# Clustered attention and a mixture of experts on one core: nine small transfers by another queue, and four edits to the plan

## The chip, the cores and the metric

The kernel runs on one core of a Trainium2 chip. A core has five engines with a queue of instructions each: TensorE (PE, matmuls), VectorE (DVE), ScalarE (ACT), GpSimd (POOL) and SyncE (SP, which here only starts transfers). Each queue is worked in order; an instruction that waits holds up everything behind it on its engine. Sixteen DMA engines move the data of all transfers. The metric is the device time of one execution in microseconds (us), the median over several runs.

## The reference, cut to what matters

The first part is attention over 4 batches, 8 heads, 768 tokens and 64 features. Each query and each key is put into one of 16 clusters, and a query sees only the keys of its own cluster. The second part sends each of the 3072 tokens to 2 of 8 experts.

```python
q_assign = argmax(q_n . c_n);  k_assign = argmax(k_n . c_n)
mask = q_assign[:, :, :, None] == k_assign[:, :, None, :]
scores = where(mask, scale * q @ k.T, -1e9)
attn = softmax(scores, axis=-1)            # the row maximum is subtracted first
x = (attn @ v).transpose(0, 2, 1, 3).reshape(3072, 512)
logits = x @ w_gate + log1p(exp(x @ w_noise)) * noise
out[token] += w[token, e] * (relu(x[token] @ w1[e]) @ w2[e])   # for the 2 best e
```

## The kernel before, in words

**Pairs.** The 32 (batch, head) matrices are worked as 16 pairs of heads, called pair 0 to 15 by the code (the first pair is pair 0). For each pair one wide operand `A` and one `B` are put together in SBUF: 128 rows that hold the high and low halves of q and k, the one-hot cluster masks in rows 64 to 79 of `A`, and the row maxima in two rows of `B`. There are three buffers of each, used in turn (`A_152`, `A_153`, `A_154` and `B_155`, `B_156`, `B_157` in the order of the instructions).

**What makes a pair ready.** `a_split` (L414 to L424) turns q and k on PE, ACT writes the high half and DVE the low half, into a tile that is called `hl` (for pair 1 `xt`). `b_place` (L490) moves the halves into `A` and `B` with ten transfers. `a_sims` to `a_eq` (L435 to L471) find the clusters, `a_mask` (L480, L482) turns them on PE and lets ACT write the mask `mk`, and `b_mask` (L502) moves `mk` into `A` with four transfers. `b_max` (L516, L519) then makes the row maxima on PE and DVE, `b_neg` (L526 to L528) joins them in `nm`, and `b_negT` (L530) turns `nm` on PE, lets ACT copy the turned maxima to `nt` and moves `nt` into `B`. For pair 0 `b_neg` and `b_negT` run once for each head, for all other pairs once for both.

**What uses it.** `scores` (L547, L548) makes one step of 128 keys: two matmuls of `A` and two of `B`, and ACT's exponential `pe`. POOL makes the low half `pl` (L559), and `values` (L580 to L586) multiplies with v four steps later. DVE scales the pair's result into `xp` (L594); for the first pair `x_first` (L627), `x_hi` (L647, ACT) and `x_lo` (L651, POOL) halve it, `x_put` (L656) stores it in DRAM and `x_turn` (L663) turns it by a transposing transfer.

**The order.** All of this is recorded step by step. A table of numbers, `AT`, gives for each piece of work the step at which it is recorded; a step is one `scores` call, twelve to a pair, and negative steps lie ahead of the first scores. What is recorded first stands first on each queue. All transfers but the gathers are started by SP through one helper, `dma` (L487), or by `nc.sync` itself. Each transfer on these queues also waits for the transfer that was recorded eight before it, whichever queue starts it, because eight completion counters are used in turn.

**Experts.** Expert by expert, `layer1` (L1267) and `layer2` (L1305) follow. While expert 0 is at work, the weights of expert 1 are loaded, DVE takes their maxima (`max_w1`, L1185), and `w1_scale` (L1163 to L1174) makes a common scale from them, with one matmul of PE in each of its two parts.

Of the kernel before, what the change touches and what calls it, by code (L numbers as in the profile page):

```python
# [9 lines left out]
F32 = mybir.dt.float32  # L10
# [19 lines left out]
    vscale=-0.667, vsplit=10.667, vstep=1.0, split=[-4.667, -3.667, -4.0, -3.333], place=-0.667,  # L30
# [1 line left out]
    bmax=9.333, neg=20.333, negT=22.0, zero=31.0, zstep=12.0, zlist=15.667, store=2.667, log=1.667, log2=3.0,  # L32
    logstep=0.667, turn=7.667, list=23.0, lstep=[2.0, 2.0, 1.0], bstep=1.0,
    gate=7.667, gstep=0.333, am=5.333, amstep=0.333, ky=4.0, cut=[13, 20], gplace=17.333,
    vd=[1, 1, 2, 3, 4, 5], sec=-6.0, qf=-4.0, place1=4.333,
    fv=[{'v': -5.0, 'vscale': 13.0, 'am': 24.333, 'amstep': 0.333, 'vsplit': 25.333, 'vstep': 2.0},
        {'v': 9.0, 'vscale': 11.667, 'am': 13.333, 'amstep': 0.333, 'vsplit': 15.0, 'vstep': 1.667}],
    thr=0.333, bmax1=14.667, bstep1=0.5)
# [6 lines left out]
class Kernel:  # L45
# [154 lines left out]
    def attention(self, ctx):  # L200
        nc, tc = self.nc, self.tc
# [17 lines left out]
        def at(step, f, *a):  # L219
            sched.setdefault(divmod(round(3 * step), 3), []).append((f, a))  # L220

        def chain(step, by, fs):
            for i, f in enumerate(fs):
                at(step + by * i, f)
# [3 lines left out]
        for p in range(NP):  # L228
            b, hp = divmod(p, H // 2)
            w = 12 * (p - 2)  # L230
            if hp == 0:
                for g in range(2):
                    at(w + T["qk"] + 24 * g + (T["qf"] if (b, g) == (0, 1) else 0), self.load_qk, b, g)
                    v = w + 24 * g
                    V = T["fv"][g] if p == 0 else T
                    at(18.667 if (b, g) == (1, 0) else v + V["v"], self.load_v, b, g)
                    for h in range(0, 4, 2):
                        at(v + V["vscale"] + V["amstep"] * h, self.v_max, b, g, h)
                    chain(v + V["am"], V["amstep"], self.v_scale(b, g))
                    for h in range(4):  # L240
                        at(v + V["vsplit"] + V["vstep"] * h, self.v_split, b, g, h)
            if p == 0:
                at(17.333, self.x_first)
            for i in range(2 if p <= NP - 4 else 0):
                hi, lo = (18.667 + 1.333 * i, 20.0 + 1.333 * i) if p == 0 else (w + 38 + 3.667 * i, w + 39.333 + 3.667 * i)
                at(hi, self.x_hi, p, i)
                at(lo, self.x_lo, p, i)
                if i:
                    at(w + 45 if p else 21.667, self.x_put, p, i)
                    if p < NP - 4:  # L250
                        at(w + 46.667 if p else 21.667, self.x_turn, p)
            P = T["first"] if p == 0 else T
            w += (0, T["sec"], T["thr"])[p] if p < 3 else 0
            for i in range(4):
                at(w + P["split"][i], self.a_split, p, i // 2, i % 2)
            if p == 0:
                at(w + P["sims"][0], self.c_turn)
            at(w + P["place"] + (T["place1"] if p == 1 else 0), self.b_place, p)
            for s in range(2):
                at(w + P["sims"][s], self.a_sims, p, s)  # L260
            for s in range(2):
                at(w + P["sum"][s], self.a_sum, p, s)
            for k, f in (("max1", self.a_max1), ("ge", self.a_ge), ("ky", self.a_ky), ("max2", self.a_max2),
                         ("eq", self.a_eq), ("mask", self.a_mask), ("bmask", self.b_mask)):
                at(w + P[k], f, p)
            if p == 0:
                for s in range(2):
                    for j in range(NJ):
                        at(w + P["bmax"][s] + P["bstep"][s] * j, self.b_max, p, s, j)
                    at(w + P["neg"][s], self.b_neg, p, s, 1)  # L270
                    at(w + P["negT"][s], self.b_negT, p, s, 1)
            else:
                w = 12 * (p - 2)
                bm, bs = (T["bmax1"], T["bstep1"]) if p == 1 else (T["bmax"], T["bstep"])
                for s in range(2):
                    for j in range(NJ):
                        at(w + bm + bs * (6 * s + j), self.b_max, p, s, j)
                at(w + T["neg"], self.b_neg, p, 0, 2)
                at(w + T["negT"], self.b_negT, p, 0, 2)
            if hp == H // 2 - 1:  # L280
                z = w + 36 + L
                if b + 1 == B:
                    continue
                at(z + (10 if b == B - 2 else 14), self.g_halves, b)
                at(z + (11 if b == B - 2 else 14.667), self.g_turn, b)
                fs = self.g_gate(b)
                k = b == B - 2
                chain(z + (13 if k else 15.333), T["gstep"] / (1 + k), fs[:self.GP])
                chain(z + (19.333 if k else 26), T["gstep"] / (1 + k), fs[self.GP:])
                for j in range(2 * NJ):  # L290
                    at(z + ((22.333 if j < 1 else 24.667 + 0.333 * j) if k else T["list"] + 8.667 + T["lstep"][b] * j), self.g_list, b, j)
# [33 lines left out]
        for t in range(min(sched)[0], z + L + 2):  # L325
# [8 lines left out]
            if 0 <= u < z:  # L334
                p, s, kc = u // 12, (u % 12) // 6, u % 6
# [148 lines left out]
        st["mk"] = mk  # L484


    def dma(self, o, i):  # L487
        self.nc.sync.dma_start(o.bitcast(F32), i.bitcast(F32))

    def b_place(self, p):  # L490
        hl, A, Bt = self.st[p]["hl"], self.A[p % 3], self.Bt[p % 3]
# [10 lines left out]
    def b_mask(self, p):  # L502
        mk, A = self.st[p]["mk"], self.A[p % 3]
        for i in range(2):
            for a in range(2):
                self.dma(A[64:80, i, :, 384 * a:384 * a + 384], mk[64 * i + 32 * a:64 * i + 32 * a + 16])

    def b_max(self, p, s, j):

# [20 lines left out]
    def b_negT(self, p, s, n):  # L530
        nc, W = self.nc, 2 * n * self.NJ
        t = self.ps()
        nc.tensor.transpose(t[:, :128], self.nm.bitcast(F32), self.ident)
        nt = self.wk.tile([32, 128], F32R, name="nt")
        nc.scalar.activation(nt[:W], t[:W, :128], AF.Copy)
        self.dma(self.Bt[p % 3][96:98, 1, s:s + n], nt[:W])


    def scores(self, p, s, kc):
# [361 lines left out]
    def experts(self, ctx):  # L901
        nc, tc, E, DM, F, N, CAP, T, TA = self.nc, self.tc, self.E, self.DM, self.F, self.N, self.CAP, self.T, self.TA
        ND, NF, NJ, b = DM // 128, F // 128, self.NJ, self.B - 1
# [8 lines left out]
        A = (0, TA * 128)  # L912
# [68 lines left out]
                self.max_w1(1, t - 1)  # L981
        self.max_w1(1, 3)
        for f in range(NF):
            if 1 <= f < 3:
                self.w1_scale(1, f - 1)
            self.prep_w2(1, f - 5)
            self.prep_x(1, f - 3)
            self.layer1(0, f, [Bs])
# [5 lines left out]
        n = CAP // 2  # L994
        for e in range(1, E):
# [5 lines left out]
            for f in range(NF):  # L1001
# [7 lines left out]
                i = f - 1 if e > 1 else f - 3  # L1009
# [355 lines left out]
```

## Time and profile before

| | |
|---|---|
| median of 3 runs | 1060.86 us (1058.88, 1060.86, 1060.91) |
| profiled execution | 1059.2 us, of which 1057.4 us span |
| PE busy | 991.9 us, 94% of the span |
| DVE, ACT, POOL busy | 664.5, 509.4 and 572.4 us |
| PE busy, 0 to 42 us | 24.98 us |
| PE busy, 42 to 125 us | 71.07 of 83 us |
| PE busy, 125 to 475 us | 333.18 of 350 us |

The span is what the profile covers; the rest of an execution lies around it. An engine's idle time counts only where the engine is the one that all others wait for. PE is that engine over most of the span, so the list of what PE waited for, and when, is read first; the timelines of the other queues show why the thing that it waited for was late. In a timeline a row may stand for several instructions (x4), its first column is the start, its second the time until the last of them ended, and what stands in brackets is idle time before the row and what ended it.

### The profile page before, as it was taken

The numbers are of one execution on the slowest core, as the hardware profiler recorded it, in microseconds if no ns is written. First come the engines' busy times: TensorE is split into PE (matmuls) and PEld (weight loads), VectorE is DVE, ScalarE is ACT, GpSimd is POOL, SyncE is SP. The second block draws the span as 40 slices with busy tenths as digits, with TensorE's granted clock in tenths as the row PEclk, the third lists the DMA queues.
The fourth block names the chain that finished last, engine by engine and source line by source line (L and its number), as shares of the span: only waits on it lengthen the run. The fifth ranks groups of instructions, "written<-read, shape, count | busy, mean of one in ns | idle before, by whom it ended". The sixth has DMA issues, their size and how long they took to land.

```text
span 1057.4 us, 21878 instructions
## 1 busy us (share of the span) xinstructions
PE 991.9 (94%) x8353; PEld 672.3 (64%) x8353; DVE 664.5 (63%) x1443; ACT 509.4 (48%) x1059; POOL 572.4 (54%) x631
## 2 busy tenths in 40 slices
PE   5788899999999999899999999999999999999994
PEld 4577899888898888785455545455454454554541
DVE  5787678787778777896645555555554565445421
ACT  3467586857685767577342415224143152331510
POOL 9167687877997799882345225243352342522211
PEclk9899999999999999999999999999999999999998
DMA  7776878787878766418396947729358294391200
GB/s 191 178 185 142 203 179 208 180 199 167 193 185 198 177 148 149 124 43 166 116 209 156 194 133 162 215 71 236 117 147 200 78 227 146 103 235 69 60 33 35
DMA packets 172878, 162.78 MB, mean 154 GB/s; under 512 B 87737, under 2 KB 151609, under 8 KB 172770
## 3 DMA queue, kind: packets, MB, share of 16 engines
q1 hardware_dynamic: 159474, 124.97, 50.4%
q0 software_dynamic: 13296, 36.38, 12.0%
q8 instruction: 67, 1.10, 0.4%
q14 instruction: 41, 0.34, 0.1%
HBM read 78.21 MB, written 26.51 MB: 99 GB/s over the span
## 4 chain that ended last, share of the span: by engine, by line
PE 65%; POOL 11%; issue 9%; DVE 7%; DMA 4%; ACT 2%; SPq 1%; POOLq 0%; DVEq 0%; ACTq 0%
PE ring L1267 22%; PE ring L1305 20%; PE ring L547 7%; POOL pl L559 4%; PE ring L516 4%; POOL tbl L867 2%; PE av L586 2%; PE av L580 2%; DVE aux L519 2%; ACT pe L548 2%; PE av L582 2%; PE ring L450 1%; PE ring L435 1%; PE ring L414 1%; DVE mm L519 1%
## 5 line engine op out<-in xcount | busy, mean ns | idle before, releaser
L559 POOL TENSOR_TENSOR pl<-pe 128x768 f16<-128x768 f32 x173 | 252.2, 1472 | 66.7 <-ACT pe L548 53.3
L1267 PE MATMUL ring<-xT,w1t 128*128 128x416 f16 (+2 forms) x1536 | 272.8, 339 | 1.9 <-DMA xT<-xg 1.9
L1305 PE MATMUL ring<-w2t,hT 128*128 128x512 f16 x1152 | 252.3, 379 | 0.6 <-ACT w2t L1151 0.5
L548 ACT ACTIVATE pe<-ring,l 128x384 f32<-128x384 f32 x384 | 201.4, 578 | 74.9 <-PE ring L547 71.2
L1267 PEld LDWEIGHTS <-w1t 128*128 128x128 f16 x1536 | 149.3, 98 | 120.7 <-issue 2.2
L1144 ACT ACTIVATE hr<-ring 128x416 f32<-128x416 f32 (+2 forms) x128 | 66.5, 519 | 273.8 <-PE ring L1267 273.8
L1305 PEld LDWEIGHTS <-hT 128*128 128x128 f16 x1152 | 112.3, 98 | 133.9 <-issue 1.1
L1317 POOL DMA_INDIRECT out<-yo,idx x52 | 62.3, 1198 | 227.7 <-DVE yo L1313 114.1
L519 DVE TENSOR_REDUCE aux<-ring 128x1 f32<-128x384 f32 x192 | 107.8, 562 | 75.3 <-PE ring L516 67.2
L547 PE MATMUL ring<-A 128*128 128x384 f32 x384 | 143.4, 373 | 2.1 <-ACT mk L482 0.7
L547 PE MATMUL ring<-B 128*128 128x384 f32 x384 | 130.0, 338 | 5.4 <-DMA B<-nt 5.4
L1147 DVE TENSOR_TENSOR hT<-hr,hT 128x416 f16<-128x416 f32 (+3 forms) x128 | 71.2, 559 | 89.0 <-ACT hT L1146 88.6
L516 PE MATMUL ring<-A 128*128 128x384 f32 x384 | 108.2, 356 | 9.1 <-ACT pe L548 4.2
L1313 DVE SCALAR_TENSOR_TENSOR yo<-ring,we,xt 128x512 f32<-128x512 f32 (+1 forms) x49 | 36.7, 748 | 123.0 <-PE ring L1305 109.2
L519 DVE TENSOR_REDUCE mm<-ring 128x1 f32<-128x384 f32 x192 | 105.0, 547 | 0.0
L1247 POOL DMA_INDIRECT xg<-xs,idx x52 | 55.7, 1072 | 84.4 <-DMA xT<-xg 74.8
L580 PE MATMUL av<-vv,pe 128*128 128x65 f16 x1152 | 97.4, 195 | 0.4 <-DVE stg L594 0.2
L582 PE MATMUL av<-vv,pe 128*128 128x64 f16 x1152 | 96.5, 192 | 0.0
L580 PEld LDWEIGHTS <-pe 128*128 128x128 bf16 x1152 | 79.7, 99 | 15.5 <-issue 10.7
L516 PEld LDWEIGHTS ring<-A 128*128 128x128 f32 x384 | 70.0, 190 | 21.7 <-ACT pe L548 12.1
L582 PEld LDWEIGHTS <-pe 128*128 128x128 bf16 x1152 | 78.1, 98 | 0.3
L547 PEld LDWEIGHTS ring<-A 128*128 128x128 f32 x384 | 73.3, 191 | 6.9 <-ACT pe L548 2.2
(224 smaller groups left out, 1381.6 us busy)
## 6 DMA issues: line engine op xcount, KB each, us to landing
stg<-in_moe_w SPq DMA_DIRECT2D x64, 512.0 KB
A<-hl SPq DMA_DIRECT2D x30, 384.0 KB
B<-hl SPq DMA_DIRECT2D x30, 384.0 KB
vt<-in_v SPq DMA_DIRECT2D x8, 768.0 KB
out<-zt SPq DMA_DIRECT2D x12, 512.0 KB
A<-hl SPq DMA_DIRECT2D x60, 96.0 KB
B<-hl SPq DMA_DIRECT2D x30, 192.0 KB
xs<-xh SPq DMA_DIRECT2D x15, 384.0 KB
```

Of the source, the lines that this page charges most:

```text
L516: nc.tensor.matmul(t, A[:, 0, s, j * 128:j * 128 + 128], A[:, 1, s, n * 384:n * 384 + 384], start=True, stop=True)
L519: nc.vector.tensor_reduce(o, t, axis=X, op=OP.max, negate=True)
L547: nc.tensor.matmul(t, M[:, 1 - qi, s, ks], M[:, qi, s, ns], start=not qi, stop=bool(qi))
L548: nc.scalar.activation(pe[:, n], t, AF.Exp, bias=self.l64[:, 0:1], scale=self.scale)
L559: (nc.vector if last else nc.gpsimd).tensor_tensor(lo, pe, hi, op=OP.subtract)
L580: nc.tensor.matmul(av[:, j, :], ph[:, js], vv[:, hh, kj, 64:129], start=(kc == 0 and j == 0), stop=False, skip_group_check=True)
L582: nc.tensor.matmul(av[:, j, :64], ph[:, js], vv[:, hh, kj, 0:64], start=False, stop=False, skip_group_check=True)
L1144: nc.scalar.activation(r[:, :n], p, AF.Relu, scale=2.0 ** -HT)
L1147: nc.vector.tensor_tensor(h1, r[:, a:b], h0, op=OP.subtract)
L1267: nc.tensor.matmul(p, self.w1t[:, wi, c, f * 128:f * 128 + 128], self.xT[e][:, c, xi, n0:n1], start=(i == 0), stop=(i == 3 * ND - 1))
L1305: nc.tensor.matmul(p, self.hT[:, hi, f, t * 128:t * 128 + 128], self.w2t[:, wi, f], start=(i == 0), stop=(i == 3 * NF - 1))
L1317: i = nc.gpsimd.indirect_dma_start(out=self.out, out_offset=bass.IndirectOffsetOnAxis(ap=en[:r], axis=0), in_=yo[:r], in_offset=None, boun ...
```

## The change

`dma` takes the engine that starts the transfer. For the first two pairs the turned maxima `nt` are started by ACT's queue instead of SP's, three transfers in all, and for the first three pairs two of the four transfers of a mask `mk` are, six in all. In the table, `place1`, by which pair 1's `b_place` is recorded, goes from 4.333 to 0. The first result is halved, stored and turned earlier (`x_first` from step 17.333 to 17, the first `x_hi` from 18.667 to 17.667, `x_put` and `x_turn` from 21.667 to 20.333). The v load of the first half of batch 1 goes from step 18.667 to 22.333, and its maxima (`v_max`) three steps later. Expert 1's `w1_scale` comes one piece of `layer1` later.

```diff
-    vd=[1, 1, 2, 3, 4, 5], sec=-6.0, qf=-4.0, place1=4.333,
+    vd=[1, 1, 2, 3, 4, 5], sec=-6.0, qf=-4.0, place1=0.0,
...
-                    at(18.667 if (b, g) == (1, 0) else v + V["v"], self.load_v, b, g)
+                    at(22.333 if (b, g) == (1, 0) else v + V["v"], self.load_v, b, g)
                     for h in range(0, 4, 2):
-                        at(v + V["vscale"] + V["amstep"] * h, self.v_max, b, g, h)
+                        at(v + V["vscale"] + V["amstep"] * h + (3 if (b, g) == (1, 0) else 0), self.v_max, b, g, h)
...
-                at(17.333, self.x_first)
+                at(17, self.x_first)
...
-    def dma(self, o, i):
-        self.nc.sync.dma_start(o.bitcast(F32), i.bitcast(F32))
+    def dma(self, o, i, by=None):
+        (by or self.nc.sync).dma_start(o.bitcast(F32), i.bitcast(F32))
...
-                self.dma(A[64:80, i, :, 384 * a:384 * a + 384], mk[64 * i + 32 * a:64 * i + 32 * a + 16])
+                self.dma(A[64:80, i, :, 384 * a:384 * a + 384], mk[64 * i + 32 * a:64 * i + 32 * a + 16],
+                         self.nc.scalar if p < 3 and a else None)
...
-        self.dma(self.Bt[p % 3][96:98, 1, s:s + n], nt[:W])
+        self.dma(self.Bt[p % 3][96:98, 1, s:s + n], nt[:W], nc.scalar if p < 2 else None)
...
         for f in range(NF):
-            if 1 <= f < 3:
-                self.w1_scale(1, f - 1)
+            if 2 <= f < 4:
+                self.w1_scale(1, f - 2)
```

SP's queue before, from the first pair's mask (`A_152<-mk`) to the second pair's place (`xt` into `A_153` and `B_156`) and mask:

```order
L488 DMA A_152<-mk 16x2x384 x4
L356 DMA qk<-in_q 128x4x384
L356 DMA qk<-in_k 128x4x384
L488 DMA B_155<-nt 2x6x128
L488 DMA A_153<-xt 64x4x384
L488 DMA A_153<-xt 32x2x384 x2
L488 DMA B_156<-xt 64x4x384
```

The same place of SP's queue now:

```order
L488 DMA A_152<-mk 16x2x384 x2
L356 DMA qk<-in_q 128x4x384
L356 DMA qk<-in_k 128x4x384
L488 DMA A_153<-xt 64x4x384
L488 DMA A_153<-xt 32x2x384 x2
L488 DMA B_156<-xt 64x4x384
```

The first turned maxima no longer stand ahead of the second pair's place, and two of the four mask transfers are gone. The order of the rest is the same.

ACT's queue before, from the first pair's mask to the third pair's splits (`hl`):

```order
L482 ACTIVATE mk<-ring,ms 128x768
L423 ACTIVATE xt<-ring 128x384 x4
L440 ACTIVATE sm<-ring 128x384 x2
L535 ACTIVATE nt<-ring 12x128
L160 ACT_TABLE_LOAD
L482 ACTIVATE mk<-ring,ms 128x768
L423 ACTIVATE hl<-ring 128x384 x4
```

The same place of ACT's queue now:

```order
L482 ACTIVATE mk<-ring,ms 128x768
L488 DMA A_152<-mk 16x2x384 x2
L423 ACTIVATE xt<-ring 128x384 x4
L440 ACTIVATE sm<-ring 128x384 x2
L536 ACTIVATE nt<-ring 12x128
L488 DMA B_155<-nt 2x6x128
L160 ACT_TABLE_LOAD
L482 ACTIVATE mk<-ring,ms 128x768
L488 DMA A_153<-mk 16x2x384 x2
L423 ACTIVATE hl<-ring 128x384 x4
```

Two transfers each now stand between a pair's mask and the next pair's splits, and one behind the turned maxima.

SP's queue before, at the first pair's store and turn (`xs<-lg`, `xt<-lg`) and the maxima of the third pair (`B_157<-nt`, which stay with SP):

```order
L488 DMA A_152<-mk 16x2x384 x4
L364 DMA vt<-in_v 128x4x384
L656 DMA xs<-lg 768x1x256
L663 DMA_TRANSPOSE xt<-lg 128x12x128
L488 DMA B_157<-nt 2x12x128
L488 DMA A_153<-hl 64x4x384
```

The same place of SP's queue now:

```order
L488 DMA A_152<-mk 16x2x384 x4
L657 DMA xs<-lg 768x1x256
L664 DMA_TRANSPOSE xt<-lg 128x12x128
L488 DMA B_157<-nt 2x12x128
L364 DMA vt<-in_v 128x4x384
L488 DMA A_153<-hl 64x4x384
```

The v load went from ahead of the store to behind the third pair's maxima. On POOL the two halvings that the store waits for went ahead of the last of that batch's v splits.

## Rows read from the trace of the kernel before

**Rows 1.** What PE waited for, 0 to 200 us: total, times, longest.

```profile
PE ring L547 <- DMA B<-nt: 5.4, 2, 3.6
PE ring L516 <- DMA A<-mk: 3.2, 2, 2.0
```

**Rows 2.** PE in order of time, parts of 20 to 125 us and 537 us.

```profile
25.32 2.90 PE L516 MATMUL ring<-A 128*128 128x384 f32 x10 [1.28 <-DMA A<-mk]
...
39.17 1.63 PE L435 MATMUL ring<-hl,wh 128*128 128x384 f32 x4
...
49.30 0.70 PE L516 MATMUL ring<-A 128*128 128x384 f32 x2 [1.96 <-DMA A<-mk]
...
62.51 0.44 PE L547 MATMUL ring<-B 128*128 128x384 f32 x1 [1.85 <-DMA B<-nt]
...
108.17 0.44 PE L547 MATMUL ring<-B 128*128 128x384 f32 x1 [3.56 <-DMA B<-nt]
...
537.00 0.27 PE L1163 MATMUL ring<-ident,wm 128*4 128x128 f32 x1 [0.83 <-DVE wm L1185]
```

**Rows 3.** SP's queue in order of time, 20 to 106 us.

```profile
21.50 2.49 SPq L488 DMA_DIRECT2D A<-mk  x4
...
32.85 0.75 SPq L488 DMA_DIRECT2D B<-nt  x1
33.66 3.02 SPq L488 DMA_DIRECT2D A<-xt  x3
...
44.26 3.66 SPq L488 DMA_DIRECT2D A<-mk  x4
...
58.71 1.43 SPq L488 DMA_DIRECT2D B<-nt  x1
...
102.42 0.58 SPq L656 DMA_DIRECT2D xs<-lg  x1
...
105.03 1.08 SPq L488 DMA_DIRECT2D B<-nt  x1
```

**Rows 4.** What SP's queue waited for, 20 to 63 us: total, times, longest.

```profile
SPq L488 <- ACT nt L535: 7.6, 1, 7.6
```

**Rows 5.** ACT in order of time, 20 to 102 us.

```profile
21.34 2.16 ACT L423 ACTIVATE xt<-ring 128x384 fp32r<-128x384 f32 x4
...
37.94 2.11 ACT L423 ACTIVATE hl<-ring 128x384 fp32r<-128x384 f32 x4
...
53.21 0.25 ACT L535 ACTIVATE nt<-ring 12x128 fp32r<-12x128 f32 x1
...
101.17 0.27 ACT L535 ACTIVATE nt<-ring 24x128 fp32r<-24x128 f32 x1 [0.30 <-PE ring L533]
```

**Rows 6.** DVE in order of time, 20 to 42 us.

```profile
21.85 2.23 DVE L424 TENSOR_TENSOR xt<-ring,xt 128x384 fp32r<-128x384 f32 x4 [2.32 <-ACT xt L423]
25.77 0.57 DVE L519 TENSOR_REDUCE aux<-ring 128x1 f32<-128x384 f32 x1 [1.68 <-PE ring L516]
...
38.46 2.18 DVE L424 TENSOR_TENSOR hl<-ring,hl 128x384 fp32r<-128x384 f32 x4 [0.65 <-ACT hl L423]
```

**Rows 7.** Issue of mask and maxima transfers, 0 to 140 us: ns, least, median, most.

```profile
L488 SPq DMA_DIRECT2D A<-mk x20: 586/592/1400, 21.5 to 127.0; - x20
...
L488 SPq DMA_DIRECT2D B<-nt x5: 663/753/1427, 32.9 to 132.4; - x5
```

**Rows 8.** Stretches: length, busy PE, PEld, DVE, ACT, POOL, granted clock, DMA share, GB/s.

```profile
49.30:52.20 2.90, 2.90 (x15) 2.70 (x16) 1.03 (x3) 1.12 (x3) 1.02 (x1) 0.78 0.87 174
...
55.00:60.00 5.00, 3.83 (x48) 2.63 (x47) 4.82 (x10) 3.07 (x6) 2.57 (x3) 1.00 0.89 207
...
63.00:73.50 10.50, 10.30 (x126) 9.50 (x124) 8.46 (x21) 8.57 (x18) 5.88 (x5) 1.00 0.72 231
108.20:112.80 4.60, 4.60 (x42) 4.01 (x43) 1.54 (x4) 2.48 (x5) 1.58 (x2) 0.63 0.88 179
```

**Rows 9.** POOL in order of time: the second low half of the first pair.

```profile
101.47 0.92 POOL L651 TENSOR_TENSOR lg<-xp,lg 128x384 f16<-128x384 f32 x1
```

More of the change, by code (lines that the diff above doesn't have):

```diff
@@ L242, in attention @@
             if p == 0:
-                at(17.333, self.x_first)
+                at(17, self.x_first)
             for i in range(2 if p <= NP - 4 else 0):
-                hi, lo = (18.667 + 1.333 * i, 20.0 + 1.333 * i) if p == 0 else (w + 38 + 3.667 * i, w + 39.333 + 3.667 * i)
+                hi, lo = (17.667 + 0.667 * i, 18.667 + i) if p == 0 else (w + 38 + 3.667 * i, w + 39.333 + 3.667 * i)
                 at(hi, self.x_hi, p, i)
@@ L248, in attention @@
                 if i:
-                    at(w + 45 if p else 21.667, self.x_put, p, i)
+                    at(w + 45 if p else 20.333, self.x_put, p, i)
                     if p < NP - 4:
-                        at(w + 46.667 if p else 21.667, self.x_turn, p)
+                        at(w + 46.667 if p else 20.333, self.x_turn, p)
             P = T["first"] if p == 0 else T
```

## The prediction, as it was put on record

> **What bounds the kernel now.** I read first how busy the engines are: PE has work in 94% of the span, and from 125 to 475 us in 333 of 350 us, while it stands for 29 us of the first 125. What the change does before 125 us can therefore show, and time gained there should be kept, since nothing behind it goes by the clock on the wall. The list of what PE waited for shows which of those waits the change aims at: twice the turned maxima (`nt` into `B`, 5.4 us) and twice a mask (`mk` into `A`, 3.2 us) [rows 1]. PE's timeline puts them at 25.32, 49.30, 62.51 and 108.17 us [rows 2]. SP's queue tells why three of these are late. At 25 us it stops for 7.6 us at the first turned maxima [rows 4], which ACT has not made yet, and the second pair's place stands behind them, so it begins at 33.66 and that pair's mask is not started before 44.26 [rows 3]. The maxima of the first pair's second head are ready at 53.46, the end of ACT's row [rows 5], but are started at 58.71, behind the third pair's place [rows 3]. The third pair's are ready at 101.44 [rows 5] and are started at 105.03, behind a store that waited until 102.42 [rows 3] for POOL's low half, which ended at 102.39 [rows 9]. So the waits are for a place in a queue more than for the moving of bytes.
>
> **The change part by part.** An issue by ACT is nowhere in this trace. By SP a mask transfer takes 0.59 us in the middle and 1.40 at most, one of maxima 0.75 and 1.43 [rows 7]. I call ACT's price c, take 0.6 for a mask (the middle of SP's rows; the operation is the same) and keep 0 (ACT goes on at once) and 1.4 as the ends.
>
> *First pair's mask, second pair's splits.* SP's four issues end at 23.99; PE gets the mask at 25.32 [rows 2, 3]. With two on each queue they end near 22.7 and the mask lands near 24.0. But ACT's splits `xt`, begun at 21.34 [rows 5], now begin at about 21.5 + 2c = 22.7. DVE's four followed 0.51 us behind and took 2.23, so they end at 25.4 instead of 24.08; the reductions, begun at 25.77 [rows 6], stand behind them and begin at 25.45. Gain 0.3; with c = 0 the mask decides and it is 1.2, with c = 1.4 DVE is done at 27.0 and 1.3 is lost.
>
> *Second pair's mask, third pair's splits.* `hl` began at 37.94, right as the mask was written [rows 5]. The mask comes 0.3 earlier and two issues stand between, so `hl` begins near 38.95 and its DVE part 1.0 later than 38.46 [rows 6]. PE's four matmuls on it, 39.17 to 40.60 with little to spare [rows 2] (the row's 1.63 covers the end of the last), then end near 41.0. First and second edit together: first scores 0.4 late (1.2 early with c = 0; 3.5 late with c = 1.4, where two delays of 2.8 add up).
>
> *Second pair's place.* It no longer stands behind the maxima and begins as soon as `xt` is there, near 25.4 instead of 33.66. It and the mask took 33.66 to 47.92 on SP [rows 3]; even if the q and k loads just ahead slow it, the pair is complete by about 43, and PE wants it at 47.34 + 0.4. So the 1.96 of [rows 2] goes whole, and what is late next is the 0.4 above. After that wait PE ran at a granted clock of 0.78 for 2.9 us [rows 8], that is 0.6 lost; I count 0.5. Moving `place1` alone moves nothing in SP's order. Sum up to here: 1.96 - 0.4 + 0.5 = 2.0, from -1.5 to 3.7.
>
> *Maxima of the second head.* Started at 53.5 they need no more than the 3.80 us from 58.71 to 62.51 [rows 2, 3], and PE arrives at 60.66, or 58.7 with the gain above. The 1.85 goes whole. Every transfer waits for the one recorded eight before it, so the last of the third pair's place now waits for these maxima; that place has 8 us more than before, which covers it. Next PE meets DVE, busy in 4.82 of 5 us there [rows 8], already in the sum.
>
> *Third pair's mask and second pair's maxima.* They bring nothing, as PE does not wait for them, and cost ACT 2c + 0.75 = 1.95 us in a stretch in which it is busy in 8.57 of 10.5 us and PE in 10.30 [rows 8]. Its idle time, 1.93, would just hold them if it lay right. I take a loss of 0.7, from 0 to 2.5 (4.2 us at the upper price less most of the idle time).
>
> *Store, turn and v load.* `x_first` goes ahead of one pair of exponentials on ACT, and POOL's second half goes ahead of a v split and one `pl`: about 98.3 instead of 102.39. Store and turn then end on SP near 101, and the maxima are started when made, 101.5 instead of 105.03. They took 3.14 us to land behind the turn, which gives 104.6, just when PE arrives (108.17 - 3.56). I count 3.2 of the 3.56. Of the clock, 0.63 over 4.6 us from 108.2 on, that is 1.7 lost [rows 8], I count 1.5. DVE's two maxima of v (1.8 us), which lay in PE's wait, come three steps later where PE does not stand: minus 0.3. The v load starts only behind these maxima, near 102.3, and its own maxima come three steps later, some 6.7 us (192 steps in about 430 us, 42 to 475), so I take no wait for it. Sum 4.4, from 2.0 to 5.0.
>
> *Scale of expert 1.* PE waits 0.83 for weight maxima at 537.00 [rows 2]; one piece of `layer1` later they are there. The halves that need the scale are made a whole `layer1` later. Gain 0.8.
>
> Total: 2.0 + 1.85 - 0.7 + 4.4 + 0.8 = 8.35 from 1059.2, the profiled execution's own time: 1050.85. The median of the runs stands 1.7 above that execution and their mean 1.0; I add 0.9 and say 1051.8.
>
> **A rule against it.** SP's rows show 5.25 us between maxima that are ready and their start, and then 3.80 until they have landed [rows 3, 5]. The Trainium skill, "DMA: Bandwidth & Descriptors", section "Rules for kernel authors", says that spreading transfers over the engines that can start them does not help, since all run on the same sixteen DMA engines, and only saves the time of issuing. The rows agree as to the 3.80, which may stay; by the rule read narrowly only nine issues would leave SP, which PE does not wait for, and the time would be the second rival's. What it does not speak of is the 5.25, which the order of one queue costs.
>
> **The rivals.**
> - *ACT's queue is the price (slower).* The six mask issues stand ahead of splits and exponentials. From c = 0.6 on, each further us of c takes 3.5/0.8 = 4.4 us from the first two pairs (from -0.4 to -3.5) less the 0.5 of the clock at the end, and about 2 in the third stretch. The gain of 8.35 is used up at c near 1.9, and at 2.3 the kernel is 2.5 us slower: 1063.5. For it: an issue at a crowded time took 1.40 and 1.43 [rows 7], and ACT has never issued here. Against it: the middle of twenty rows is 0.59.
> - *Early pairs bring nothing, transfers share what there is.* The second pair's place meets the q and k loads, the maxima meet the third pair's place, and the third pair's maxima land no earlier than the store and turn allow. Then only parts of the waits go: 1.0 + 0.9 + 1.8 of 1.96, 1.85 and 3.56, no clock, ACT's 1.1 against it, 0.8 from the scale: 3.4 less, 1056.7. Against it: 53.5 + 3.80 is 57.3, ahead of PE.
> - *The store is not earlier.* If POOL's second half comes only at about 101, being behind ACT, the last part brings 0.5 instead of 4.4: 1055.7. For it: that half waits for ACT's high half, which still has exponentials and a v split ahead of it. Against it: POOL's order.
>
> **How the numbers follow.** Forecast, within 1048.5 and 1054, 62%. Shared transfers 13%, store not earlier 12%, ACT's upper price with the rest as forecast (about 1055.5) 7%, ACT slower than before 6%. A measurement of this kernel tells some 0.2%, 2.1 us, from no change. Forecast and the middle cases lie nearly all over 2.1 us faster: 0.88 with the tails taken off; within it 0.07; slower 0.05. Range for 8 in 10: low 1048, from all prices at 0 (3.7 + 1.85 + 5.0 + 0.8 = 11.35, 1048.8) and a little under; high 1057, which takes in the middle cases.
>
> **What would show it.** Right: the second pair's place on SP from 25 or 26 us; no PE wait for `A<-mk` near 48 and none for `B<-nt` near 59; the maxima of the third pair started within 0.5 us of ACT's row, and at most 0.5 of 3.56 left; ACT's issue rows near 0.6; no wait of L1163 near 530 (537 less the gain). Wrong: issue rows of over 1 us on ACT and PE waiting for `hl`, `xt` or `pe` behind them; a new wait for a v load near 108; the first scores after 43.5; or a late wait after 125 us that takes back what was gained.

## The result, and the profile after

The changed kernel takes 1050.66 us in the median of 6 runs (1048.91 to 1052.78), the kernel before beside it 1060.12 (1058.88 to 1062.55). The ratio is 0.991, with a 95% interval from 0.989 to 0.9929. Forecast were 1051.8 us; the profiled execution took 1051.9 us, of which 1050.1 us span. The sum was right; which of its terms were right is another matter, and most of what follows is about that.

What PE waited for from 0 to 200 us, after (total, times, longest), as far as it answers to [rows 1]:

```profile
PE ring L517 <- DVE hl L424: 1.4, 1, 1.4
PE ring L435 <- ACT xt L423: 0.8, 1, 0.8
PE ring L435 <- ACT hl L423: 0.6, 1, 0.6
PE ring L517 <- DMA A<-mk: 0.5, 1, 0.5
```

Of the 5.4 us for `B<-nt` nothing is left, and of the 3.2 us for masks none of the two old waits; ahead of the matmuls for the first pair's maxima PE still stands 0.57 us (the row at 24.83 below), which the profile puts down to POOL's fill of `B`. The 0.5 us for a mask is a new wait at 177 us; five other traces here have one of 0.2 to 0.7 us between 185 and 480 us, the two of before have none. In place of the old waits PE waits 2.8 us for splits, `xt` and `hl`, which stand behind the new issues on ACT. SP's queue after, answering to [rows 3]:

```profile
20.66 1.22 SPq L488 DMA_DIRECT2D A<-mk  x2
...
25.35 2.16 SPq L488 DMA_DIRECT2D A<-xt  x3
...
39.40 1.35 SPq L488 DMA_DIRECT2D A<-mk  x2
...
96.28 0.58 SPq L657 DMA_DIRECT2D xs<-lg  x1
96.90 1.89 SPq L664 DMA_TRANSPOSE xt<-lg  x1
99.49 0.77 SPq L488 DMA_DIRECT2D B<-nt  x1
```

The second pair's place starts at 25.35 instead of 33.66, and the store at 96.28 instead of 102.42 (some 2 us of that were gained earlier, by the table below). POOL's second half of the first pair ends just ahead of the store (answers to [rows 9]):

```profile
95.34 0.92 POOL L652 TENSOR_TENSOR lg<-xp,lg 128x384 f16<-128x384 f32 x1
```

What an issue costs, 0 to 140 us (ns: least, median, most), answers to [rows 7]:

```profile
L488 SPq DMA_DIRECT2D A<-mk x14: 585/592/1037, 20.7 to 119.7; - x14
L488 ACTq DMA_DIRECT2D A<-mk x6: 636/686/857, 20.7 to 62.5; - x6
...
L488 ACTq DMA_DIRECT2D B<-nt x3: 673/679/1184, 32.4 to 71.5; - x3
```

A mask costs ACT 0.69 us against 0.59 on SP, near the 0.6 that was taken for c. What it holds up is seen in ACT's order of time, answering to [rows 5]:

```profile
38.14 1.34 ACTq L488 DMA_DIRECT2D A<-mk  x2
39.66 1.64 ACT L423 ACTIVATE hl<-ring 128x384 fp32r<-128x384 f32 x4 [1.60 <-DMA A<-xt]
...
53.20 0.25 ACT L536 ACTIVATE nt<-ring 12x128 fp32r<-12x128 f32 x1
53.48 0.67 ACTq L488 DMA_DIRECT2D B<-nt  x1
...
61.85 1.53 ACTq L488 DMA_DIRECT2D A<-mk  x2
```

`hl` starts at 39.66 instead of 37.94. The row puts the 1.60 us before it down to a transfer, but 1.34 of them are the two issues of the row above. The maxima of the second head go out 0.03 us after they are made. PE, answering to [rows 2]:

```profile
24.83 3.30 PE L517 MATMUL ring<-A 128*128 128x384 f32 x10 [0.57 <-POOL B L345]
...
36.21 0.82 PE L480 MATMUL ring<-identb,oh 128*128 128x128 bf16 x6 [3.04 <-DVE oh L471]
...
40.21 1.92 PE L435 MATMUL ring<-hl,wh 128*128 128x384 f32 x4 [0.61 <-ACT hl L423]
41.92 2.12 PE L517 MATMUL ring<-A 128*128 128x384 f32 x6
43.84 0.52 PE L548 MATMUL ring<-A 128*128 128x384 f32 x1
...
49.62 0.51 PE L517 MATMUL ring<-A 128*128 128x384 f32 x2
...
66.63 0.70 PE L517 MATMUL ring<-A 128*128 128x384 f32 x2 [1.41 <-DVE hl L424]
```

The mask wait at 49 us is gone. But the four matmuls on `hl` come 1.04 us later than 39.17 [rows 2], and the first scores at 43.84; first scores after 43.5 were one of the prediction's signs of being wrong, and so was PE waiting for `hl` and `xt`. Two windows of before and after tell of the clock (columns as in [rows 8]); first before:

```profile
40.00:45.00 5.00, 4.55 (x22) 3.48 (x20) 4.53 (x13) 2.21 (x6) 1.41 (x1) 0.93 0.95 208
50.00:55.00 5.00, 5.00 (x27) 4.90 (x26) 3.30 (x8) 2.52 (x6) 1.94 (x3) 0.66 0.88 176
```

Then after, with a third that answers to [rows 8]:

```profile
40.00:45.00 5.00, 4.79 (x14) 4.30 (x14) 4.47 (x10) 2.07 (x6) 0.00 (x0) 0.50 0.54 95
50.00:55.00 5.00, 4.78 (x30) 3.99 (x28) 4.14 (x10) 3.35 (x8) 4.39 (x4) 1.00 0.88 203
108.20:112.80 4.60, 4.60 (x60) 4.49 (x56) 4.53 (x11) 2.22 (x5) 3.76 (x3) 1.00 1.01 226
```

The half clock (1.2 GHz) after the mask wait and after the wait for the third pair's maxima is gone: 1.00 where it was 0.66 and 0.63. A new stretch of it, 0.50 instead of 0.93, lies on the first scores.

### The profile page after: what moved, and what is told of

Its sections match the earlier page's. It is cut to its first block, busy times and chain, and to the rows that moved or that the text cites. A ratio compares the mean times of both kernels' runs of the same rounds, so it can differ in the third digit from the quotient of the medians.

```text
span 1050.1 us, 21874 instructions
## 1 busy us (share of the span) xinstructions
PE 992.0 (94%) x8353; PEld 671.7 (64%) x8353; DVE 663.7 (63%) x1443; ACT 508.8 (48%) x1059; POOL 574.0 (55%) x631
## 4 chain that ended last, share of the span: by engine, by line
PE 42%; issue 7%; POOL 2%; DMA 1%; ACT 1%; DVE 1%; SPq 0%; POOLq 0%; ACTq 0%
PE ring L1268 20%; PE ring L1306 19%; PE ring L1296 1%; POOL out L1318 1%; POOL xt L1281 1%; PE ring L1299 1%; PE ring L1173 0%; DMA xg<-xs,idx 0%; DMA xT<-xg 0%; DMA xs<-xh 0%; PE ring L692 0%; POOL xh L652 0%; DMA out<-yo,idx 0%; PE ring L700 0%; POOL ent L846 0%
```

## The experiments

**How the traces are compared.** There are 384 exponentials in the same order in every kernel here. The start of the same one is taken in two traces; a change from one to the next tells where time is lost or gained, whatever lay ahead. The marks are those that start at 42.45, 63.0, 76.7, 101.6 and 127.7 us in before's trace. The first column is worked out within one trace: from PE's turn of the second pair's mask (`oh`, 36.21 in the rows above) to the first exponential. The other columns are differences from before's trace in us, minus is a gain; the last is the difference of the whole span.

| kernel | `oh` to first exp | 42 to 63 | 63 to 77 | 77 to 102 | 102 to 128 | end, whole |
|---|---|---|---|---|---|---|
| before | 6.31 | | | | | |
| changed | 8.51 | -6.0 | +2.4 | -0.7 | -5.0 | -7.3 |
| changed again | 8.42 | -6.1 | +2.4 | -0.7 | -5.0 | -9.4 |
| maxima only | 5.54 | -6.5 | +1.3 | 0.0 | +0.8 | -3.4 |
| masks only | 9.04 | -3.2 | +2.3 | 0.0 | +0.1 | +4.2 |
| no mask | 6.05 | -6.5 | +1.3 | -0.7 | -5.0 | -9.2 |
| masks 1 and 2 | 8.73 | -6.1 | +1.1 | -0.7 | -5.0 | -4.0 |
| mask 1 | 5.93 | -6.5 | +1.3 | -0.7 | -5.0 | -10.8 |
| mask 1 again | 6.25 | -6.5 | +1.3 | -0.7 | -5.0 | -9.0 |
| mask 2 | 8.91 | -6.3 | +1.2 | -0.7 | -5.1 | -3.1 |
| mask 2 behind | 6.74 | -6.5 | +1.3 | -0.7 | -5.0 | -9.3 |
| store only | 5.97 | +0.3 | +1.5 | -0.7 | -5.0 | -4.7 |
| scale only | 6.24 | 0.0 | 0.0 | 0.0 | 0.0 | +1.3 |
| before again | 6.20 | +0.2 | 0.0 | 0.0 | -0.1 | +5.8 |

The stretches from 42 to 128 us repeat within a few tenths, but for two that a half clock lengthens in one trace alone (the +0.8 of the maxima alone, 101.1 to 108.0 us, and part of the store's +1.5). What lies ahead of `oh` (35.4 to 37.8 us) and behind 128 us differs by up to several us between traces, also of one kernel; so single edits are judged by the stretches and whole kernels by the timed ratios.

**Maxima alone** (before, with three transfers of `nt` on ACT).

```diff
-        self.dma(self.Bt[p % 3][96:98, 1, s:s + n], nt[:W])
+        self.dma(self.Bt[p % 3][96:98, 1, s:s + n], nt[:W], nc.scalar if p < 2 else None)
```

> The kernel before, with one part of the change: the turned maxima of the first two pairs are started by ACT's queue; masks, store, v load and scale as before. My theory (the waits come from the order of SP's queue): the second pair's place starts near 25 us, PE's waits at 49.3 (1.96) and 62.5 (1.85) go and a little of the clock, with three issues of 0.7 us on ACT beside idle time: 4 us faster than before, 1056. The wait of 3.6 us near 108 stays. Rival (the pair is late because its mask is issued in a row of four, or because bytes are slow): at most 2 us faster, and a wait for the mask stays near 48.

Measured: 1058.19 us (10 runs), before on that chip 1062.59; ratio 0.996 [0.9944, 0.9975]. That is 4.4 us, where the theory said 4. SP's queue in this run:

```profile
25.32 2.32 SPq L488 DMA_DIRECT2D A<-xt  x3
...
38.77 3.57 SPq L488 DMA_DIRECT2D A<-mk  x4
```

The place starts where it does in the changed kernel, so the three maxima alone open SP's queue. Of PE's waits in [rows 1] the one for the third pair's maxima is left (40 to 130 us):

```profile
PE ring L547 <- DMA B<-nt: 3.6, 1, 3.6
```

The stretch from 42 to 77 us is 6.5 - 1.3 = 5.2 us shorter.

**Masks alone** (before, with half of three masks on ACT).

```diff
-                self.dma(A[64:80, i, :, 384 * a:384 * a + 384], mk[64 * i + 32 * a:64 * i + 32 * a + 16])
+                self.dma(A[64:80, i, :, 384 * a:384 * a + 384], mk[64 * i + 32 * a:64 * i + 32 * a + 16],
+                         self.nc.scalar if p < 3 and a else None)
```

> The kernel before, with one part of the change: two of the four mask transfers of the first three pairs are started by ACT; everything else as before. My theory: SP still stands at the first maxima, so no wait goes but some tenths of the first mask, and six issues of 0.65 us delay the splits and exponentials behind them: 1 to 3 us slower than before, 1062. Rival (masks land sooner and that is worth something by itself): 1 to 2 us faster, 1058.5.

Measured: 1063.4 us (12 runs), before on that chip 1062.59; ratio 1.0008 [0.9992, 1.0024]. Neither the gain of the rival nor the 1 to 3 us of loss of the theory can be told from nothing. In the trace 2.7 us are lost ahead of the first exponential (9.04 against 6.31) and 2.3 from 63 to 77 us; the 3.2 gained between go with the mask wait at 49 us and the half clock behind it (1.00 over 50 to 55 us), which are gone, as PE arrives later.

**No mask on ACT** (the changed kernel without the masks).

```diff
-                         self.nc.scalar if p < 3 and a else None)
+                         None)
```

> The changed kernel with all masks started by SP again; maxima, store, v load and scale as changed. My theory: the masks on ACT are a loss, above all the third pair's (2.0 us by the two traces): 2 to 3 us faster than the changed kernel, 1048. Rival (masks on two queues carry part of the gain): 1 to 2 us slower than the changed kernel, 1052.

Measured: 1050.58 us (5 runs), before on that chip 1062.59; ratio 0.9886 [0.9866, 0.9906]. PE in this run, and its window (columns as in [rows 8]):

```profile
36.14 0.82 PE L480 MATMUL ring<-identb,oh 128*128 128x128 bf16 x6 [3.04 <-DVE oh L471]
...
39.17 1.44 PE L435 MATMUL ring<-hl,wh 128*128 128x384 f32 x4
...
41.64 0.34 PE L548 MATMUL ring<-A 128*128 128x384 f32 x1
```

```profile
40.00:45.00 5.00, 4.55 (x23) 3.48 (x22) 4.74 (x12) 2.45 (x6) 1.47 (x1) 0.98 0.79 148
```

With the same start of `oh` (36.14 and 36.21) the scores come at 41.64 against 43.84 with the masks. The 2.2 us are 1.04 that PE's matmuls on `hl` are late and, for the rest, the clock: it is at 0.98 here and at 0.50 there. That the whole kernel is 2 to 3 us faster than the changed one, as expected, these runs do not show: 0.9886 [0.9866, 0.9906] and 0.991 [0.989, 0.9929] overlap.

**First and second pair's masks** (the third back on SP; the same line with `p < 2`).

> The changed kernel with the third pair's mask alone started by SP again. My theory: the 1.4 us for which PE waits for the next pair's splits behind the two issues on ACT goes, with some tenths more: 1.5 to 2 us faster than the changed kernel, 1049. Rival (that wait is hidden or comes back at the next step): the same as the changed kernel within 0.5 us.

Measured: 1053.35 us (6 runs), before on that chip 1062.59; ratio 0.9906 [0.988, 0.9932]. The stretch 63 to 77 us goes back from +2.4 to +1.1, so the third mask costs 1.3 us there; that is the wait of 1.41 at 66.63 above. The ratio does not tell this kernel from the changed one; its profiled execution lost 3.9 us behind 128 us, where it has no edit that the changed one lacks.

**First pair's mask, and second pair's, each alone** (the same line with `p == 0`, and with `p == 1`).

> The changed kernel with the second and third pairs' masks back on SP: only the first pair's mask is half on ACT. In the kernel with all masks on SP the first scores came 0.3 us earlier than before, the scores at 63 us 6.8 earlier, at 77 us 5.4. Theory A (each mask costs what stands behind it on ACT): first scores between 0.4 late and 0.4 early, 6 us or more gained at 63. Theory B (the late splits keep PE at the low clock): the low clock lasts to about 45 us instead of 40, first scores 2 us late, 4 us gained at 63.

> The changed kernel with the first and third pairs' masks back on SP: only the second pair's mask is half on ACT. Theory A (two issues stand ahead of the third pair's splits): first scores 1 to 1.5 us late, low clock to 45 us, 4 us gained at 63. Theory B (the first mask did it): first scores as before, low clock to 40 us, 6.5 us gained at 63.

Measured, one run each: 1048.37 and 1056.21 us. From `oh` to the first exponential it is 5.93 with the first mask and 8.91 with the second. PE waits for the split in the second:

```profile
39.77 1.92 PE L435 MATMUL ring<-hl,wh 128*128 128x384 f32 x4 [1.01 <-ACT hl L423]
```

So the second mask is the dear one. The 7.8 us between the two times are not its price: from `oh` to the first exponential it costs 3.0, at 128 us its trace is 2.3 us behind the other (its `oh` came 0.6 earlier), and 5.4 more were lost between 128 us and the end. Against before's trace it lost 5.4 between 458 and 477 us alone, with a half clock from 461.1 to 464.5 us that before's trace does not have.

**The changed kernel once more, and the first mask timed** (the same two kernels, on one chip).

> The changed kernel once more, with another profile. If its late start is a cost of the masks on ScalarE's queue, it shows again: the low clock lasts to about 45 us, TensorE waits for ScalarE's split near 40 us and for VectorE's near 66 us, the exponential that before's trace has at 130 us starts 7 to 8 us earlier, and the ratio is near 0.991. If the first trace was an accident, the low clock ends near 40 us as in the run with the first pair's mask alone, and 10 us or more are gained at 130 us.

> Of the masks, only the first pair's second half goes by ScalarE's queue; the rest is as in the changed kernel. My theory: the second and third pairs' halves cost 3 to 4 us through late splits and the clock, so this one is 3 to 4 us faster than the changed kernel on the same chip, ratio near 0.988. The rival, that the difference of the single looks is scatter: the same ratio as the changed kernel within 0.001.

Measured: changed 1051.1 us (6 runs), ratio 0.9918 [0.9899, 0.9937]; with the first mask alone 1048.04 (5 runs), ratio 0.9874 [0.9854, 0.9893]. The new trace of the changed kernel repeats the first (8.42, -6.1, +2.4), so its late start is no accident. The two intervals do not meet, and 3.1 us is what the second and third masks cost together; by the stretches it is 2.2 to 3.0 and 1.1 to 1.3. This version beats both kernels. From the one without any mask it is not told apart: 0.9886 and 0.9874 overlap.

**Second mask behind the splits** (the changed kernel with the third mask on SP and ACT's part of the second recorded after the four splits `hl`; `part` chooses one half).

```diff
+                at(-2.667, self.b_mask, 1, 1)
...
-    def b_mask(self, p):
+    def b_mask(self, p, part=None):
...
-            for a in range(2):
+            for a in range(2) if part is None else (part,):
...
-                         self.nc.scalar if p < 3 and a else None)
+                         self.nc.scalar if p < 2 and a else None)
```

> The third pair's mask is back on SP, and ScalarE's half of the second pair's mask is recorded behind the third pair's four splits. Theory A, that its place ahead of the splits is what costs: first scores 0.3 to 0.6 us earlier than before, low clock to about 40 us, 6.5 to 7 us gained at 63 us. Theory B, that the mask lands late or that the issue on ScalarE costs wherever it stands: 4 to 5 us gained at 63 us, or a new wait of TensorE for the mask near 48 us.

Measured, one run: 1049.93 us. ACT in this run:

```profile
38.49 1.52 ACT L427 ACTIVATE hl<-ring 128x384 fp32r<-128x384 f32 x3
...
40.24 1.29 ACTq L492 DMA_DIRECT2D A<-mk  x2
```

PE in this run:

```profile
36.74 0.82 PE L484 MATMUL ring<-identb,oh 128*128 128x128 bf16 x6 [3.04 <-DVE oh L475]
...
39.77 1.63 PE L439 MATMUL ring<-hl,wh 128*128 128x384 f32 x4
...
42.83 0.44 PE L552 MATMUL ring<-A 128*128 128x384 f32 x1
...
47.85 0.51 PE L521 MATMUL ring<-A 128*128 128x384 f32 x2
```

The same two issues, 1.29 us, now cost little: no wait for `hl`, none for the mask at 47.85, and 6.74 us from `oh` to the first exponential instead of 8.51 (8.73 with the same two masks ahead of the splits). This speaks for theory A: what costs is the place ahead of the splits. In absolute time the first scores were 0.9 late and not 0.3 to 0.6 early, since `oh` itself came 0.6 later in this trace, which the expectation did not allow for; and 5.4 us were gained by 63 us, not 6.5.

**Store, turn and v load alone** (before with the six lines of the change's table that belong to it; three are shown).

```diff
-                    at(18.667 if (b, g) == (1, 0) else v + V["v"], self.load_v, b, g)
+                    at(22.333 if (b, g) == (1, 0) else v + V["v"], self.load_v, b, g)
...
-                at(17.333, self.x_first)
+                at(17, self.x_first)
...
-                    at(w + 45 if p else 21.667, self.x_put, p, i)
+                    at(w + 45 if p else 20.333, self.x_put, p, i)
```

> The kernel before, with one part of the change: the first pair's store and turn earlier, the v load and its maxima later. My theory: the third pair's maxima are started when ACT has made them, PE's wait of 3.56 near 108 goes with the low clock behind it, and by 130 us the program stands 4.5 to 5.5 us earlier than before; the waits at 49.3 and 62.5 stay. Rival (these maxima land only when the store and the turn ahead of them have): 2 us or less, with a wait for them left.

Measured, one run: 1054.5 us. SP in this run:

```profile
98.30 0.58 SPq L656 DMA_DIRECT2D xs<-lg  x1
...
101.52 0.70 SPq L488 DMA_DIRECT2D B<-nt  x1
```

The store is 4.12 us earlier than 102.42 and the maxima 3.51 earlier than 105.03 [rows 3]. From 77 to 128 us 5.7 us are gained, as in every kernel with this edit; 128 us is reached 5.0 us earlier than in before's trace, as the theory had it. (Its +1.5 from 63 to 77 us goes with a half clock from 63.2 to 66.6 us in its trace.)

**Scale alone** (before with the last line pair of the change's diff).

```diff
-            if 1 <= f < 3:
-                self.w1_scale(1, f - 1)
+            if 2 <= f < 4:
+                self.w1_scale(1, f - 2)
```

> The kernel before, with the scale of expert 1 one piece of layer1 later and nothing else. My theory: the wait of 0.83 near 537 goes and 0.8 us is kept to the end. Rival (the next wait there, 0.75 for xT near 563, grows by as much): nothing is kept, the start of expert 1 stands where it stood.

Measured, one run: 1060.48 us, before beside it 1059.67. What PE waited for from 525 to 550 us:

```profile
PE ring L1172 <- DVE gmax L1166: 0.9, 1, 0.9
PE ring L1267 <- DMA xT<-xg: 0.5, 1, 0.5
```

The wait of 0.83 at L1163 [rows 2] is gone, and one of 0.9 stands at L1172, where DVE's maximum of the next part is late. By the starts of PE's matmuls the stretch from 488 to 567 us is 0.7 us shorter than in before's first trace, but so it is by 0.4 to 0.6 in the traces of the maxima, the masks and the store alone, which lack this edit, and it is 0.2 longer in the second trace of before (next experiment). So 0.8 us kept is not shown, and not ruled out. Over all traces it is no plainer: with the edit the wait of `w1_scale` (at one of its two matmuls) is 0.9, 1.1 and 1.5 in three and absent in six; without it 0.8, 1.0, 1.0, 1.2 and 0.2. The wait for gathered tokens (`xT<-xg`) beside it varies between 0 and 2.7; both together are 0.2 to 2.7 with the edit and 1.0 to 2.7 without.

**Before once more**, for a second trace.

> The kernel before, unchanged, for a second trace of it. All comparisons of starts so far rest on one trace of before; between its 491 and 567 us runs with and without the scale edit came out 0.6 to 2.1 us shorter. Theory: that stretch was 1 us slow in the first trace by chance, so this trace is also about 1 us shorter there, while its starts up to 475 us agree with the first trace within 1 us. Rival: it takes the same time there within 0.3 us; then the runs without the scale edit gained by something that they have in common.

Measured: 1065.01 us, before beside it 1065.14. The stretch between 491 and 567 us is the rival's: the same within 0.2 us, not 1 us shorter. So the shorter ones there may have something in common; the traces of the maxima, the masks and the store alone have no wait for gathered tokens there, where the two of before have 1.9 and 2.2, and why stays open. Up to 475 us the two traces do not agree within 1 us as the theory had it; they differ by 1.5 us ahead of the first scores. PE's row and window there (25 to 32 us, columns as in [rows 8]), both from the second trace:

```profile
25.62 3.54 PE L516 MATMUL ring<-A 128*128 128x384 f32 x10 [2.94 <-DMA A<-mk]
...
25.00:32.00 7.00, 6.38 (x22) 6.11 (x22) 4.74 (x10) 0.49 (x1) 1.06 (x2) 0.52 0.74 230
```

The wait for the first pair's mask was 2.94 instead of 1.28 [rows 2], but PE's work behind it began only 0.30 later. The rest is the clock: it was at 0.52 from 25 to 32 us, where the first trace has 1.00, and the ten matmuls took 3.54 us instead of 2.90. From 42 to 128 us nothing differs by over 0.2; between 458 and 488 us another 3.7 were lost. Two traces of one kernel differ by more than most of the single edits bring. The differences end by 568 us: from there to the end all fourteen traces take the same time within 0.1 us.

`place1` has no share: with it put back to 4.333 in the changed kernel, the five queues hold the same instructions in the same order.

## Why the prediction was right, and which steps of it were not

*First pair's mask, second pair's splits.* Gain 0.3 forecast. It can't be told: `oh` of the second pair starts at 35.54 to 36.74 us in seven traces with this edit, and at 35.38 to 37.76 in seven without. PE's matmuls for the first maxima start 0.49 earlier (24.83 against 25.32 [rows 2]), but `oh` of the second pair no earlier (36.21 against 36.14). In the changed kernel PE waits 0.8 for `xt`; the step had `xt` late, but reckoned only with DVE behind it.

*Second pair's mask, third pair's splits.* This step failed. It had the splits begin 1.0 late and the first scores 0.4 late, and called PE's row at 39.17 one "with little to spare". `hl` came 1.7 late, 39.66 against 37.94, by 1.34 of issues and the gap behind them; PE's matmuls on it came 1.04 late. And PE, at half clock since before 35 us, stayed there until about 45 instead of 41 us, so that everything up to the scores ran at 0.50: from `oh` to the first exponential 2.1 and 2.2 us are lost in the two traces of the changed kernel, 2.4 to 2.7 in the other three that have this mask ahead of the splits. The price of an issue was right (0.69 against 0.6); that the clock rises later behind the late splits was not in the sum. The prediction had also named this sign against itself, first scores after 43.5; they came at 43.84.

*Second pair's place and the maxima of the second head.* Forecast 1.96 + 0.5 + 1.85 = 4.3; measured 5.2 net (6.5 to 63 us, of which 1.3 is given back by 77 us). Both waits went whole, as said. The term that was mis-sized is the clock: I looked at the 2.9 us after the wait, where 0.78 makes 0.6 us, but the half clock lasted longer. Over 50 to 55 us it was 0.66 with PE busy all the time, which is 5 x 0.34 = 1.7. The same stretches (42 to 63, 63 to 77 us by the marks), first before, then with no mask on ACT (columns as in [rows 8]):

```profile
42.45:63.05 20.60, 15.15 (x101) 12.16 (x100) 14.39 (x34) 10.10 (x21) 11.30 (x9) 0.92 0.84 180
63.05:76.70 13.65, 13.45 (x173) 12.49 (x172) 11.63 (x28) 10.59 (x21) 8.78 (x7) 1.00 0.63 186
...
42.19:56.29 14.10, 13.31 (x101) 10.81 (x99) 13.08 (x32) 9.88 (x20) 9.84 (x9) 1.00 0.87 194
56.29:71.27 14.98, 14.59 (x173) 12.39 (x172) 13.36 (x32) 10.69 (x21) 10.05 (x9) 1.00 0.67 181
```

Up to 63 us the 6.5 are 4.7 of PE's idle time (3.8 of it the two waits) and 1.8 of busy time, nearly all of it the clock (0.92 over 20.6 us is 1.7). Of the 1.3 that come back by 77 us, 1.1 are PE's busy time for the same 173 matmuls at full clock (14.59 against 13.45), while DVE's busy time grows from 11.63 to 13.36. Why was not tried; the step named DVE as next.

*Third pair's mask, second pair's maxima.* Forecast a loss of 0.7 within 0 to 2.5; measured 1.1 (2.4 against 1.3), as PE's wait of 1.41 for `hl` at 66.63. The mechanism holds; the cause is the mask, since the kernels with the maxima on ACT and this mask on SP show the 1.3 and no more.

*Store, turn and v load.* Forecast 4.4; measured 5.7 (0.7 and 5.0). POOL's half was forecast 4.1 earlier, and the store alone is 4.12 earlier. The whole 3.56 went, not 3.2, and the whole 1.7 of the clock, not 1.5; the other 0.7 lies between 77 and 102 us, and was not followed further.

*Scale of expert 1.* 0.8 was forecast from the one row at L1163, without asking when DVE's `gmax` would be there for the next matmul. The wait at L1163 is gone in every trace with the edit, as said, but in three of nine one of 0.9 to 1.5 stands at the next matmul, and a gain is not shown.

The sum held because the errors had opposite signs: 1.9 too little for the second pair's mask, 0.4 for the third and up to 0.8 for the scale on the one side, 0.9 on the maxima and 1.3 on the store on the other. That they nearly cancel is luck, and what lies behind 128 us, where two traces of one kernel differ by 1.6 and 4.2 us, could have moved the total by more than the 1.1 us between forecast and median. The trace of the changed kernel says -7.3 and its repetition -9.4 for a forecast of -8.35, and the timed medians say 9.5.

**The rule against it.** Three small transfers on another queue, no byte less, gave 0.996 [0.9944, 0.9975] by themselves, and six more masks there gave 1.0008 [0.9992, 1.0024]. The Trainium skill, "DMA: Bandwidth & Descriptors", section "Rules for kernel authors", says that spreading transfers over the issuing engines does not help bandwidth and only saves issue time. For the masks the runs agree: with the maxima gone and no mask on ACT, PE waited for a mask only in the first pair (1.5 us), and each issue that SP was spared, ACT paid for. For the maxima more than issue time was saved: what they had cost was the wait at the head of SP's queue, 7.6 us [rows 4].

*The rivals.* The first, ACT's queue as the price, had the right place and not the size: 3.1 us are lost there, of the 12.3 that the kernel with the first mask alone gains (1060.29 - 1048.04). (Its 3.5/0.8 = 4.4 should be 3.1/0.8 = 3.9, since the first two pairs go from 0.4 to 3.5 late; the c at which the gain is used up stays near 1.9.) The second (early pairs bring nothing) is out: 5.2 us came from them. The third (the store no earlier) is out by 98.30.

## What to carry to other kernels

A transfer that waits for its data blocks the queue that starts it: move the one that waits, not those that could go at once, and put it on the engine that makes its data, where it stands ready by the time it is reached. An issue on a working engine costs its full time to whatever stands behind it, so give it a place behind the work that the critical engine needs next: the same two issues cost 2.2 us ahead of the splits and 0.4 behind them (8.51 and 6.74 against 6.31; the 6.74 is from one trace, and kernels with this mask all on SP range from 5.54 to 6.31). When a wait is removed, look in the trace how long the clock stays low after it, and count that to the end.

## What the runs showed of the hardware

- In the changed kernel's trace an issue on ACT's queue took 0.64 to 0.86 us for a mask of 48 KB and 0.67 to 1.18 for maxima, and nothing of ACT ran beside it; on SP the masks took 0.59 in the middle in the same stretch. Over all traces the two on ACT range from 0.60 to 1.25 and from 0.62 to 1.38.
- Where PE at half clock waited 0.55 to 1.15 us for `hl`, the full clock came back at 44.1 to 45.6 us, in all five traces with this mask ahead of the splits; in the nine others at 39.3 to 42.3.
- One kernel's traces differ by 1.5 us in what lies ahead of 42 us and by some 4 us behind 128 us, while the 85 us between repeat within 0.2 in the three kernels traced twice (before, changed, first mask): an edit worth 1 us can be judged in its own stretch where whole times can't.
